# Attention tiles 5 to 8 of a forgetting-attention and mixture kernel: scores computed once with keys along the row, P transposed by DMA, the tail's products alternating between batches

## The chip, the cores and the metric

One core of a Trainium2 chip runs the whole kernel. The metric is the device time of one execution in microseconds (us). Three runs of the kernel before gave 1038.94, 1040.11 and 1040.14 us, median 1040.11. Engines: PE (matrix products, with PEld, its weight loads), DVE (VectorE), ACT (ScalarE), POOL (GpSimd) and SP (here mainly the queue that issues DMAs).

## The reference

Causal attention with a forget bias, then a mixture of eight experts whose routing weights are balanced in eight rounds, then a bilinear layer:

```python
B, H, S, D = 2, 8, 576, 64
scores = (q @ k.T) / sqrt(D)
cum = cumsum(maximum(s, 0))                       # along the sequence
scores = where(causal, -1e9, scores + minimum(-(cum_q - cum_k), 0))
attn = exp(scores - max(scores)); attn /= sum(attn) + 1e-9
x = (attn @ v) laid out as (1152 tokens, 512)
P = exp(x @ w_gate - max); 8 rounds of row and column normalising
x = sum over e of P[:, e] * (relu(x @ w1[e]) @ w2[e])        # 8 experts
out = ((x @ w_a) * (x @ w_b)) @ w_out
```

## The kernel before

The 1152 tokens are nine tiles of 128 rows. Tiles 0 to 3 are batch 0, tiles 4 to 7 batch 1 (576 = 4 x 128 + 64), and tile 8, the tail, holds the last 64 rows of both batches, batch 0 on partitions 0 to 63 and batch 1 on 64 to 127. The order of the tiles is 0, 4, 1, 2, 3, 5, 6, 7, 8. Nearly every factor is held as a sum of two f16 numbers (hi and lo), and a product is three f16 products: hi hi, hi lo, lo hi.

Tiles 0 and 4 take `first_tile` (f32 products of 64 rows, L1033, four heads in each half of the array's rows). The others take this path:

- `k_prep` and `q_prep` write split keys and queries, and DMA transposes on SP's queue (L792, L810, L816) turn them into `ka1`, `ka2`, `b3` and `b4`, with head dimension and bias terms on the partitions.
- `row_max` computes approximate scores with queries on the partitions and keys along the row: one product a head over all its keys (L838; in the tail L855 and L868), and a mask product on the diagonal block (L823). DVE takes the row maxima (L842, L859, L871).
- `shift` (L885 to L896) turns the maxima into two more rows of `b3`: three small DVE operations, a transpose on PE, two copies by ACT.
- `probs` computes the scores a second time, now with keys on the partitions, so that P comes out transposed: two products of 128 queries for each block of 128 keys and head (L932, L933), four blocks in one bank `st`. ACT takes exp (L942). In tiles 3 and 5 to 8 (`SEL`) POOL zeroes what lies above the diagonal (L946). The result is split into hi (L954, L953) and lo (L956, L957) in one of five `pt` buffers. `pv` multiplies by v: three products of 64 or 65 columns a block (L975 to L977), into `xp`. The last column of v is 1 and gives the row sum.
- `x_tile` divides by the sum, splits and transposes by DMA (L1098) into `xt`. `gate_item` computes the eight routing logits of a tile in 12 products (L1135 to L1137).

The tail runs `probs` for one batch after the other, its last keys as blocks of 64 rows.

Expert 0 (`e0_tile`: L1179 to L1181 and L1199 to L1201) runs between these pieces, tile by tile, whenever the attention's next piece isn't ready. After the last attention tile, `switch` gives the attention's memory to experts 1 to 7. The weights of expert 1, in two stage buffers by then, are squared and summed (L593) and split only after it, since their units lie in that memory.

The order on each engine is static. `Graph.schedule` plans it when the kernel is built: each operation has a cost, an engine or a choice of engines, its dependencies and a rank, and of those that can start soonest on an engine the lowest rank goes first. `GROUPS` holds an offset for the ranks of each group ("m5" is row_max of tile 5, "p5" its probs). An engine works through its list in order and waits where an operand isn't there yet. SP's queue is in order as well.

Of the kernel before, what the change touches and what calls it, by code (L numbers as in the profile page):

```python
# [252 lines left out]
def forgetting_attention_moe_bilinear_kernel(  # L253
# [50 lines left out]
    wgs = const.tile([128, 2, KD, E], F16, name="wgs")  # L304
# [110 lines left out]
    mx8 = ap.tile([128, H], F32, name="mx8")  # L415
    ush = ap.tile([128, H], F32, name="ush")
# [91 lines left out]
    def vone(b):  # L508
        g.add("POOL", 200, lambda: nc.gpsimd.memset(vs[b][:, :, :, 64:66], 1.0), w=[("vone", b)] + ([("v1r", j) for j in range(NBLK)] if b else []), rank=0.7)
# [60 lines left out]
    def w_prep(name, e, unit_ids, rank, fine=False, rel=0.0, zs=None, srank=None):  # L570
# [7 lines left out]
        for u in range(2):  # L578
            z = next_stage() if zs is None else zs[u]
            sts.append(z)  # L580
            sv = stage[z].rearrange("p (c f) -> p c f", c=4)
            src = src0[u].rearrange("(c p) f -> p c f", p=128)
            step = 4 // npc
            for c in range(0, 4, step):
                g.add("DMA" if fine else "SP", 650 * step, lambda qu=nc.sync, sv=sv, src=src, c=c, step=step: qu.dma_start(
                    out=sv[:, c:c + step], in_=src[:, c:c + step]),
                    w=[("st", z, cc) for cc in range(c, c + step)], rank=rank + u * 0.01, rel=rel)
# [43 lines left out]
    def v_prep(b, rank, rel=0.0):  # L631
# [8 lines left out]
        g.add("DVE", 60, lambda: nc.vector.memset(mxs, 0.0), w=[("vm", b)], rank=0)  # L640
        for j in range(NBLK):
            kr = 128 if j < NJ else vrem
            g.add("DMA", 1080 * kr / 128, lambda q, j=j, kr=kr: q.dma_start(
                out=sv[j][0:kr].rearrange("p (h d) -> p h d", h=H),
                in_=v[b, :, j * 128:j * 128 + kr, :].rearrange("h s d -> s h d")), w=svk[j], rank=rank, rel=rel)
            g.add("ACT", 800, lambda j=j, kr=kr: sumsq(mxs[0:kr, j:j + 1], sv[j][0:kr], junk[0:kr]), r=svk[j] + [("vm", b)], w=[("vmx", b, j)], rank=rank)
# [7 lines left out]
        for j in range(NBLK):  # L654
            kr = 128 if j < NJ else vrem
# [14 lines left out]
    def qk_load(name, t, b, rank, rel=0.0):  # L670
        src, dst, keys = rawof[name]
        for (tt, p0, rows, bb, s0) in segs:
            if tt == t and bb == b:
                g.add("DMA", 1080 * rows / 128, lambda qu, p0=p0, rows=rows, s0=s0: qu.dma_start(
# [3 lines left out]
    SK, SQ, IK, IQ, ESC, AL, IAL, CF, NAF, APL, TA, TB = range(12)  # L678
# [4 lines left out]
    def scales(b, rank):  # L683
# [38 lines left out]
        def consts2():  # L722
# [11 lines left out]
            nc.vector.scalar_tensor_tensor(out=col(APL), in0=col(NAF), scalar=2.0 ** 10, in1=col(APL), op0=ALU.mult, op1=ALU.add)  # L734
            r = slice(64 * b, 64 * b + 64)
            nc.vector.tensor_copy(cst[r, 2, 0:TB + 1], cst[r, b, 0:TB + 1])
# [244 lines left out]

    fsc = {}

    def first_load(t, rank):
        b = t // NJ
        for name in "kq":
            qk_load(name, t, b, rank)
        g.add("DMA", 1080, lambda q: q.dma_start(out=vf[:, :, 0:64], in_=v[b, :, 0:128, :].rearrange("h s d -> s h d")), w=["vf"], rank=rank + 0.02)
# [7 lines left out]
    def first_tile(t, rank):  # L996
# [3 lines left out]
        for gg in range(2):  # L1000
# [9 lines left out]
            g.add("PE", 1065, pre, r=["idb", "msk", "ones", ("bd", b, gg)], w=[("ss", y)], rank=rank, rows=0.2)  # L1010
        zt = []
        for src, keys, scale, pi in ((kraw[t], krk[t], 1.0, 2), (qraw[t], qrk[t], qk_scale, 3)):
# [8 lines left out]
            g.add("PE", 535, tr, r=keys + ["id32"], w=[("st", z)], rank=rank, rows=0.3)  # L1021
            g.add(("ACT", "DVE"), (600, 660), (lambda z=z, pi=pi, scale=scale: nc.scalar.activation(ptf[pi], st[z], AF.Copy, scale=scale),
                  lambda z=z, pi=pi, scale=scale: nc.vector.tensor_scalar(ptf[pi], st[z], scale, None, op0=ALU.mult)),
                  r=[("st", z)], w=[("pt", pi, 0), ("pt", pi, 1)], rank=rank)
        for gg in range(2):
            y, z = ys[gg], stc[0] % NST
            stc[0] += 1

            def mm(gg=gg, y=y):
                for w in range(4):  # L1030
                    r = slice(64 * gg, 64 * gg + 64)
                    c = slice(w * 128, w * 128 + 128)
                    nc.tensor.matmul(ss[y][:, w * 128:(w + 1) * 128], lhsT=ptf[3][r, c], rhs=ptf[2][r, c], start=False, stop=True, skip_group_check=True)  # L1033

            g.add("PE", 900, mm, r=[("pt", pi, x) for pi in (2, 3) for x in range(2)], w=[("ss", y)], rank=rank, rows=0.3)
# [12 lines left out]
            g.add("PE", 535, tr, r=[("p32", gg), "id32"], w=[("st", z)], rank=rank, rows=0.3)  # L1048
# [7 lines left out]
            g.add("PE", 860, pv, r=[("pt", gg, 0), ("pt", gg, 1), "vf", "vfone"], w=[("xp", gg)], rank=rank, rows=0.3)  # L1056
# [4 lines left out]
    def x_tile(t, rank):  # L1061
# [17 lines left out]
        if t in FIRST:  # L1079
# [7 lines left out]
            g.add("PE", 535, tr, r=["id32"], w=[("st", z)] + xbk, rank=rank, rows=0.3)  # L1087
# [16 lines left out]
    def gate_prep(rank):  # L1104
# [6 lines left out]
        g.add("ACT", 215, lambda: hi_of(wgs[:, 0].rearrange("p c e -> p (c e)"), wf, sx), r=["wgn", ("wgsx",)], w=["wgs"], rank=rank)  # L1111
        g.add("DVE", 160, lambda: lo_of(nc.vector, wgs[:, 1].rearrange("p c e -> p (c e)"), wf, sx, wgs[:, 0].rearrange("p c e -> p (c e)")),
# [15 lines left out]
    def gate_item(t):  # L1128
# [4 lines left out]
        def mm():  # L1133
            for c in range(KD):
                nc.tensor.matmul(p, lhsT=xt[:, 0, c, sl], rhs=wgs[:, 0, c], start=(c == 0), stop=False)  # L1135
                nc.tensor.matmul(p, lhsT=xt[:, 0, c, sl], rhs=wgs[:, 1, c], start=False, stop=False)
                nc.tensor.matmul(p, lhsT=xt[:, 1, c, sl], rhs=wgs[:, 0, c], start=False, stop=(c == KD - 1))  # L1137

        g.add("PE", 310, mm, r=[("xt", t), "wgs"], w=mbk(m), rank=frank())
        g.add("DVE", 195, lambda: nc.vector.tensor_scalar(logit[:, t], p, isx[:, t:t + 1], gi_[0], op0=ALU.mult, op1=ALU.mult),  # L1140
# [132 lines left out]
    for t in TORD[2:]:  # L1273
# [15 lines left out]
        g.at = f"m{t}"  # L1289
        mxk = row_max(t, zb, u0)  # L1290
        shift(t, zb, mxk, u0)
        g.at = f"p{t}"
        probs(t, zb, u0 + 2)
# [779 lines left out]
LAND = 1100.0  # L2073
SEL = (3, 5, 6, 7, 8)
GROUPS = {
# [54 lines left out]
```

## Time and profile before

| | |
|---|---|
| Median of three runs | 1040.11 us |
| The profiled execution's own time | 1039.97 us |
| Its span from first to last instruction | 1038.2 us |
| Busy: PE, DVE, ACT, POOL | 98%, 74%, 53%, 9% of the span |
| DMA | 114.29 MB, mean 110 GB/s |

PE's busy time is an upper figure: its products are pipelined, so each one's listed duration (about 0.2 us) overlaps the next one's. What a product costs PE when products follow each other is the distance between the starts. The span has three stretches: up to about 125 us loads, preparations and the first attention tiles; to about 224 us the rest of attention with expert 0 between; then experts 1 to 7 and the bilinear layer.

### The profile page before, as it was taken

What the parts mean: (1) busy time and instruction counts of PE and PEld (TensorE: products, weight loads), DVE (VectorE), ACT (ScalarE), POOL (GpSimd) and SP (SyncE); (2) the same over time, 40 slices, a digit from 0 to 9 for tenths busy, and PEclk for the clock granted to TensorE, in tenths of its full rate; (3) what the DMA queues carried; (4) which work ended last, traced back from release to release, by engine and by line L of the source; (5) the groups of instructions that cost most, each with busy time, mean ns of one, the idle gap of its engine ahead of it and who ended that gap; (6) DMA issues with size and microseconds to landing.
All of it is one profiled execution on the core that took longest, in us unless ns stands there. A gap on an engine that the chain in (4) does not pass through costs nothing.

```text
span 1038.2 us, 19277 instructions
## 1 busy us (share of the span) xinstructions
PE 1015.9 (98%) x7802; PEld 651.0 (63%) x7802; DVE 773.2 (74%) x1615; ACT 545.1 (53%) x1015; POOL 92.4 (9%) x152
## 2 busy tenths in 40 slices
PE   7798999999999999999999999999999999999998
PEld 4577777866546745754764674576477464455777
DVE  7798976369966898894889789389978796666402
ACT  5767757556235635653663773466355454545220
POOL 0356822000000000000000000000000000000000
PEclk9999999999999999999999999999999999999999
DMA  9986941022023235313334522332544542222202
GB/s 231 201 138 104 166 80 23 12 83 81 1 82 122 82 122 195 110 63 122 123 107 149 198 76 75 124 120 89 203 162 168 158 92 82 88 101 97 82 21 71
DMA packets 123370, 114.29 MB, mean 110 GB/s; under 512 B 84736, under 2 KB 99072, under 8 KB 118672
## 3 DMA queue, kind: packets, MB, share of 16 engines
q1 hardware_dynamic: 120144, 112.25, 37.6%
q10 hardware_dynamic: 3136, 0.81, 0.5%
q8 instruction: 61, 1.00, 0.4%
q14 instruction: 29, 0.24, 0.1%
HBM read 79.22 MB, written 21.23 MB: 97 GB/s over the span
## 4 chain that ended last, share of the span: by engine, by line
PE 91%; DMA 3%; DVE 3%; SPq 2%; issue 1%; ACT 0%; POOL 0%; DVEq 0%; ACTq 0%; POOLq 0%
PE yb L1201 10%; PE yb L1200 10%; PE yb L1199 10%; PE yb L1585 5%; PE yb L1587 5%; PE yb L1586 5%; PE mb L1585 3%; PE mb L1587 3%; PE mb L1586 3%; PE yb L1816 2%; PE yb L1817 2%; PE yb L1815 2%; PE mb L1156 2%; PE mb L1158 2%; PE mb L1157 2%; PE mb L1816 1%
## 5 line engine op out<-in xcount | busy, mean ns | idle before, releaser
L1199 PE MATMUL yb<-wun,ht 128*128 128x512 f16 x504 | 191.0, 379 | 0.0
L1200 PE MATMUL yb<-wun,ht 128*128 128x512 f16 x504 | 191.0, 379 | 0.0
L1201 PE MATMUL yb<-wun,ht 128*128 128x512 f16 x504 | 191.0, 379 | 0.0
L1201 PEld LDWEIGHTS <-ht 128*128 128x128 f16 x504 | 49.3, 98 | 59.5
L1200 PEld LDWEIGHTS <-ht 128*128 128x128 f16 x504 | 49.3, 98 | 58.4
L1199 PEld LDWEIGHTS <-ht 128*128 128x128 f16 x504 | 49.3, 98 | 58.4
L381 DVE SCALAR_TENSOR_TENSOR wun<-stage,sc,wun 128x1024 f16<-128x1024 f32 (+1 forms) x70 | 76.6, 1117 | 8.6 <-ACT wun L367 8.4
L1585 PE MATMUL yb<-sx,wun 128*128 128x288 f16 x288 | 82.4, 286 | 0.0
L1586 PE MATMUL yb<-sx,wun 128*128 128x288 f16 x288 | 82.4, 286 | 0.0
L1587 PE MATMUL yb<-sx,wun 128*128 128x288 f16 x288 | 82.4, 286 | 0.0
L1645 DVE SCALAR_TENSOR_TENSOR acc<-yb,pe,acc 128x512 f32<-128x512 f32 x63 | 47.3, 750 | 41.5 <-PE yb L1201 40.7
L1586 PEld LDWEIGHTS <-wun 128*128 128x128 f16 x672 | 65.8, 98 | 17.8 <-issue 0.3
L1585 PEld LDWEIGHTS <-wun 128*128 128x128 f16 x672 | 65.8, 98 | 17.6
L367 ACT ACTIVATE wun<-stage,sc 128x1024 f16<-128x1024 f32 (+1 forms) x64 | 63.1, 1021 | 25.2 <-PE yb L1201 21.1
L1587 PEld LDWEIGHTS <-wun 128*128 128x128 f16 x672 | 65.8, 98 | 16.6
L364 ACT ACTIVATE jk<-stage 128x1024 f16<-128x1024 f32 x52 | 54.8, 1054 | 32.8 <-DMA stage<-in_moe_w_dram 32.2
L367 ACT ACTIVATE wun<-h,sc 128x1024 f16<-128x1024 f32 x36 | 40.8, 1144 | 43.7 <-DVE h L1436 18.5
L1595 ACT ACTIVATE ht<-yb 128x288 f16<-128x288 f32 x96 | 39.1, 408 | 33.1 <-PE yb L1587 32.5
L1585 PE MATMUL mb<-xt,wun 128*128 128x288 f16 x192 | 54.9, 286 | 0.1
L1587 PE MATMUL mb<-xt,wun 128*128 128x288 f16 x192 | 54.9, 286 | 0.0
L1586 PE MATMUL mb<-xt,wun 128*128 128x288 f16 x192 | 54.9, 286 | 0.0
L1179 PE MATMUL mb<-xt,wun 128*128 128x128 f16 x288 | 52.3, 225 | 0.0
(486 smaller groups left out, 2692.4 us busy)
## 6 DMA issues: line engine op xcount, KB each, us to landing
stage<-in_moe_w_dram SPq DMA_DIRECT2D x26, 1024.0 KB, 5.2
md<-wun SPq DMA_DIRECT2D x18, 1024.0 KB, 4.3
wun<-md SPq DMA_DIRECT2D x12, 1024.0 KB, 4.9
stage<-in_moe_w_dram SPq DMA_DIRECT2D x24, 256.0 KB, 4.6
mr<-in_moe_w_a_dram SPq DMA_DIRECT2D x12, 512.0 KB, 6.3
mr<-in_moe_w_b_dram SPq DMA_DIRECT2D x12, 512.0 KB, 4.0
mr<-in_moe_w_out_dram SPq DMA_DIRECT2D x12, 512.0 KB, 4.8
stage<-md SPq DMA_DIRECT2D x5, 1024.0 KB, 4.8
```

Of the source, the lines that this page charges most:

```text
L364: nc.scalar.activation(out, src, AF.Square, accum_out=dst)
L367: nc.scalar.activation(hi, src, AF.Copy, scale=scale)
L381: eng.scalar_tensor_tensor(out=lo, in0=src, scalar=scale, in1=hi, op0=ALU.mult, op1=ALU.subtract)
L1179: nc.tensor.matmul(p, lhsT=wh, rhs=xh, start=(c == 0), stop=False)
L1199: nc.tensor.matmul(pp, lhsT=hh, rhs=wh, start=(f == 0), stop=False)
L1200: nc.tensor.matmul(pp, lhsT=hh, rhs=wl, start=False, stop=False)
L1201: nc.tensor.matmul(pp, lhsT=hl, rhs=wh, start=False, stop=(f == KF - 1))
L1585: nc.tensor.matmul(p, lhsT=wh, rhs=xh, start=first and ch == 0, stop=False, skip_group_check=True)
L1586: nc.tensor.matmul(p, lhsT=wh, rhs=xl, start=False, stop=False, skip_group_check=True)
L1587: nc.tensor.matmul(p, lhsT=wl, rhs=xh, start=False, stop=ch == 1, skip_group_check=True)
L1595: g.add("ACT", 52 + 120 + CN / 1.2, lambda: nc.scalar.activation(hh(), src(), AF.Relu), r=bk, w=k0, rank=-5)
L1645: g.add("DVE", 663, lambda t=t, z=z: nc.vector.scalar_tensor_tensor(out=acc[:, t], in0=yb[z], scalar=pe[:, t, e:e + 1], in1=acc[:, t], op0 ...
```

## The change

- Tiles 5 to 8 (`ROWP`) take a new `row_path` in place of `row_max`, `shift` and `probs`. The full scores (both products) are computed once, with keys along the row, and masked in PSUM. DVE takes the maximum and a bias from it, ACT takes exp a head at a time with that bias, and the result is split into hi and lo. Both halves of a group go through one DMA transpose on SP into a "room", a part of `raw` that held q or k. `pv` reads from there. Scores alternate over four banks (`ss`, `st`).
- In the tail, each piece has both batches' products next to each other, in the two halves of the array's columns. The last 64 keys get a group of their own for all heads. In `vs` they are placed on the partition half that a head's transposed P has, with zeros elsewhere: so their v comes in two DMAs a batch, after a zero fill.
- `first_tile` issues its 16 products as one piece that alternates between the two row halves, where it had two pieces of 8.
- `gate_item` takes 8 products for 12 (hi times both halves of the gate in one product of 16 columns); DVE adds the halves.
- Costs in the plan (loads 1080 to 1200, some of PE's) and all offsets in `GROUPS` are new. The rest of the kernel is as before.

```diff
+ROWP = (5, 6, 7, 8,)
 ...
+        if t in ROWP:
+            row_path(t, zb, u0)
+        else: (row_max, shift, probs as before)
 ...
+    def row_path(t, zb, rank):
+        kc = NJ * 128 if tail else 128 * (j + 1)
+        G = 512 // kc
+        rooms = [x for x in (0, 2, 3, 4, 5, 1) if x in (0, 2) or x == 1 and tail or 3 <= x <= t - 2]
+        lhs = ((b3[zb], ka2), (b4[z4], ka1))
+        def parts(pi, p3, flat, room, rk, m):
+            hi, lo, src = flat[:, 0:m], flat[:, m:2 * m], p32[p3][:, 0:m]
 ...
+            g.add("SP", 1600 * m / 512, lambda: nc.sync.dma_start_transpose(out=room[:, 0:2 * m]..., in_=flat[:, 0:2 * m]), ...)
 ...
+            def mm(h0_=h0_, sb=sb):
+                for w in range(G):
+                    if tail:
+                        for x, (q_, ka) in enumerate(lhs):
+                            for bb in range(B):
+                                nc.tensor.matmul(sb[half[bb]], lhsT=q_[:, h, half[bb]], rhs=ka[:, h, bb * NJ * 128:(bb + 1) * NJ * 128], ...)
+                        continue
+                    for x, (q_, ka) in enumerate(lhs):
+                        nc.tensor.matmul(ps, lhsT=q_[:, h], rhs=ka[:, h, b * NJ * 128:b * NJ * 128 + kc], ...)
+                    mask_s(ps[:, kc - 128:kc], 128, 128)
+            def top(hs=hs, sb=sb):
+                nc.vector.tensor_reduce(out=mxr[:, t, hs], in_=sb..., op=ALU.max)
+                if tail:
+                    nc.vector.tensor_tensor(out=mxr[:, t, hs], in0=mxr[:, t, hs], in1=mx8[:, hs], op=ALU.max)
+                nc.vector.tensor_scalar(nbi[:, t, hs], mxr[:, t, hs], cc(ci, NES), 14.0 * math.log(2.0), op0=ALU.mult, op1=ALU.add)
+            def ex(h0_=h0_, sb=sb, p3=p3):
+                for w in range(G):
+                    nc.scalar.activation(p32[p3][:, c], sb[:, c], AF.Exp, scale=cc(ci, ESC), bias=nbi[:, t, h0_ + w:h0_ + w + 1])
+                def pv(h=h, w=w, room=room):
+                    for i in range(NJ if tail else j + 1):
+                        for lo, vl in ((0, 0), (0, 1), (1, 0)):
+                            for bb in range(B) if tail else (b,):
+                                nc.tensor.matmul(o, lhsT=p, rhs=vs[bb][:, i, h, 66 * vl:66 * vl + 65 - vl], ...)
 ...
     # first_tile
+        def mm():
+            for w in range(4):
+                for gg in range(2):
+                    nc.tensor.matmul(ss[ys[gg]][:, w * 128:(w + 1) * 128], lhsT=ptf[3][r, c], rhs=ptf[2][r, c], ...)
 ...
     # gate_item
+                nc.tensor.matmul(mb[m][:, 0:2 * E], lhsT=xt[:, 0, c, sl], rhs=wgs[:, c].rearrange("p z e -> p (z e)"), ...)
+                nc.tensor.matmul(p, lhsT=xt[:, 1, c, sl], rhs=wgs[:, c, 0], ...)
 ...
     # v_prep
+        g.add("POOL", 500, lambda: nc.gpsimd.memset(sv[NJ], 0.0), ...)
+            for y in range(1 if j < NJ else 2):
+                rows = slice(0, 128) if j < NJ else slice(64 * y, 64 * y + 64)
+                hs = slice(0, H) if j < NJ else slice(y, H, 2)
```

## Rows read from the trace of the kernel before

**Rows 1.** The page's busy time of each engine, share and instructions.
```profile
PE 1015.9 (98%) x7802; PEld 651.0 (63%) x7802; DVE 773.2 (74%) x1615; ACT 545.1 (53%) x1015; POOL 92.4 (9%) x152
```

**Rows 2.** The page's chain of work that ended last, by engine.
```profile
PE 91%; DMA 3%; DVE 3%; SPq 2%; issue 1%; ACT 0%; POOL 0%; DVEq 0%; ACTq 0%; POOLq 0%
```

**Rows 3.** Stretches: length, busy us (instructions) by engine, clock, DMA share, GB/s.
```profile
60.00:112.00 52.00, 47.62 (x654) 36.97 (x654) 46.59 (x123) 38.46 (x69) 35.13 (x46) 1.00 0.73 116
...
112.00:200.00 88.00, 86.09 (x1478) 69.25 (x1475) 61.27 (x120) 55.98 (x96) 27.64 (x43) 1.00 0.39 72
125.00:200.00 75.00, 75.00 (x1267) 58.95 (x1266) 48.44 (x100) 46.27 (x80) 16.81 (x30) 1.00 0.28 51
```

**Rows 4.** PE in order of time, tile 7: start, duration, line, product.
```profile
148.65 0.38 PE L838 MATMUL ss<-ka,b 128*128 128x512 f16 x1
148.86 0.22 PE L823 MATMUL ss<-msk,idb 128*128 128x128 f16 x1
148.92 0.38 PE L838 MATMUL ss<-ka,b 128*128 128x512 f16 x1
...
157.38 0.22 PE L932 MATMUL st<-b,ka 128*128 128x128 f16 x1
...
158.21 0.22 PE L933 MATMUL st<-b,ka 128*128 128x128 f16 x1
```

**Rows 5.** PE in order of time, the tail's pieces and what follows each.
```profile
151.12 0.22 PE L855 MATMUL ss<-ka,b 128*64 128x64 f16 x2
...
151.75 0.23 PE L1179 MATMUL mb<-xt,wun 128*128 128x128 f16 x1
...
158.36 0.62 PE L868 MATMUL ss<-ka,b 128*64 128x512 f16 x4
158.92 0.23 PE L1179 MATMUL mb<-xt,wun 128*128 128x128 f16 x1
...
181.87 0.20 PE L932 MATMUL st<-b,ka 128*128 128x64 f16 x1
...
182.44 0.21 PE L975 MATMUL xp<-vs,pt 64*64 64x65 f16 x1
...
183.85 0.21 PE L975 MATMUL xp<-vs,pt 64*64 64x65 f16 x1
...
184.05 0.22 PE L975 MATMUL xp<-vs,pt 128*64 128x65 f16 x1
...
184.55 0.21 PE L975 MATMUL xp<-vs,pt 64*64 64x65 f16 x1
```

**Rows 6.** PE in order of time, the gate of tile 8 and what follows.
```profile
199.75 0.17 PE L1135 MATMUL mb<-wgs,xt 128*128 128x8 f16 x1
...
200.06 0.38 PE L1199 MATMUL mb<-wun,h 128*128 128x512 f16 x1
```

**Rows 7.** PE in order of time, eight products of a first tile.
```profile
43.04 2.07 PE L1033 MATMUL ss<-pt,pt 64*128 64x128 f32 x8
```

**Rows 8.** PE's waits for DMAs from 60 to 205 us: total, times, longest.
```profile
PE ss L838 <- DMA b<-qa: 0.3, 1, 0.3
...
PE mb L1135 <- DMA xt<-xhl: 0.2, 1, 0.2
```

**Rows 9.** Transposes of the keys: issue ns min/median/max on SP's queue, and issue to landing.
```profile
L792 SPq DMA_TRANSPOSE ka<-kn x18: 1232/1276/2606, 54.0 to 131.9; - x18
...
DMA to landing us min/median/max: 3.1/3.9/6.2
```

**Rows 10.** DVE from 112 to 205 us, a small operation: busy, mean ns, idle before.
```profile
L1071 DVE TENSOR_SCALAR rs<-xp 128x4 f32<-128x4 f32 x10 | 1.6, 160 | 5.9 <-PE xp L977 5.9
```

**Rows 11.** After the last attention tile: ACT, DVE and PE in order of time.
```profile
199.39 0.63 ACT L593 ACTIVATE wun<-stage 128x512 f16<-128x512 f32 x1 [2.72 <-DMA xt<-xhl]
...
211.50 3.39 DVE L381 SCALAR_TENSOR_TENSOR wun<-stage,sc,wun 128x512 f16<-128x512 f32 x5
...
224.65 0.34 PE L1156 MATMUL mb<-xt,wun 128*128 128x384 f16 x1
```

More of the change, by code (lines that the diff above doesn't have):

```diff
@@ L415, in forgetting_attention_moe_bilinear_kernel @@
     mx8 = ap.tile([128, H], F32, name="mx8")
+    nbi = ap.tile([128, NTL, H], F32, name="nbi")
     ush = ap.tile([128, H], F32, name="ush")
@@ L508, in vone, with f @@
     def vone(b):
-        g.add("POOL", 200, lambda: nc.gpsimd.memset(vs[b][:, :, :, 64:66], 1.0), w=[("vone", b)] + ([("v1r", j) for j in range(NBLK)] if b else []), rank=0.7)
+        def f():
+            nc.gpsimd.memset(vs[b][:, :, :, 64:66], 1.0)
+            for y in range(2):
+                nc.gpsimd.memset(vs[b][64 - 64 * y:128 - 64 * y, NJ, y::2, 64:66], 0.0)
+        g.add("POOL", 400, f, w=[("vone", b)] + ([("v1r", j) for j in range(NBLK)] if b else []), rank=0.7)
     vone(0)
@@ L640, in v_prep @@
         g.add("DVE", 60, lambda: nc.vector.memset(mxs, 0.0), w=[("vm", b)], rank=0)
+        g.add("POOL", 500, lambda: nc.gpsimd.memset(sv[NJ], 0.0), w=svk[NJ] + [svk[NJ][0] + ("b",)], rank=rank, rel=rel)
         for j in range(NBLK):
[L642 to L645, printed above, removed]
+            kr = 128
+            for y in range(1 if j < NJ else 2):
+                rows = slice(0, 128) if j < NJ else slice(64 * y, 64 * y + 64)
+                hs = slice(0, H) if j < NJ else slice(y, H, 2)
+                g.add("DMA", 1200 if j < NJ else 500, lambda q, j=j, rows=rows, hs=hs: q.dma_start(
+                    out=sv[j][rows].rearrange("p (h d) -> p h d", h=H)[:, hs],
+                    in_=v[b, hs, j * 128:j * 128 + rows.stop - rows.start, :].rearrange("h s d -> s h d")), w=svk[j] if y == 0 else [svk[j][0] + ("b",)], rank=rank, rel=rel)
+            if j == NJ:
+                svk[j] = [svk[j][0], svk[j][0] + ("b",)]
             g.add("ACT", 800, lambda j=j, kr=kr: sumsq(mxs[0:kr, j:j + 1], sv[j][0:kr], junk[0:kr]), r=svk[j] + [("vm", b)], w=[("vmx", b, j)], rank=rank)
@@ L673, in qk_load @@
             if tt == t and bb == b:
-                g.add("DMA", 1080 * rows / 128, lambda qu, p0=p0, rows=rows, s0=s0: qu.dma_start(
+                g.add("DMA", 1200 if rows == 128 else 900, lambda qu, p0=p0, rows=rows, s0=s0: qu.dma_start(
                     out=dst[t][p0:p0 + rows].rearrange("p (h d) -> p h d", h=H), in_=src[b, :, s0:s0 + rows, :].rearrange("h s d -> s h d")),
                     w=keys[t] if rows == 128 else [keys[t][b]], rank=rank, rel=rel)
-    SK, SQ, IK, IQ, ESC, AL, IAL, CF, NAF, APL, TA, TB = range(12)
+    SK, SQ, IK, IQ, ESC, AL, IAL, CF, NAF, APL, TA, TB, NES, LNC = range(14)
     def cc(ci, i, r=slice(0, 128)):
@@ L987, in first_load @@
             qk_load(name, t, b, rank)
-        g.add("DMA", 1080, lambda q: q.dma_start(out=vf[:, :, 0:64], in_=v[b, :, 0:128, :].rearrange("h s d -> s h d")), w=["vf"], rank=rank + 0.02)
+        g.add("DMA", 1200, lambda q: q.dma_start(out=vf[:, :, 0:64], in_=v[b, :, 0:128, :].rearrange("h s d -> s h d")), w=["vf"], rank=rank + 0.02)
     def first_scale(t, rank):
@@ L1008, in pre @@
                 nc.tensor.matmul(ss[y], lhsT=ones[0:H], rhs=bd[b][gg], start=False, stop=False, skip_group_check=True)
-            g.add("PE", 1065, pre, r=["idb", "msk", "ones", ("bd", b, gg)], w=[("ss", y)], rank=rank, rows=0.2)
+            g.add("PE", 1300, pre, r=["idb", "msk", "ones", ("bd", b, gg)], w=[("ss", y)], rank=rank, rows=0.2)
         zt = []
@@ L1024, in first_tile @@
                   r=[("st", z)], w=[("pt", pi, 0), ("pt", pi, 1)], rank=rank)
+        def mm():
+            for w in range(4):
+                for gg in range(2):
+                    r = slice(64 * gg, 64 * gg + 64)
+                    c = slice(w * 128, w * 128 + 128)
+                    nc.tensor.matmul(ss[ys[gg]][:, w * 128:(w + 1) * 128], lhsT=ptf[3][r, c], rhs=ptf[2][r, c], start=False, stop=True, skip_group_check=True)
+        g.add("PE", 1100, mm, r=[("pt", pi, x) for pi in (2, 3) for x in range(2)], w=[("ss", y) for y in ys], rank=rank, rows=0.2)
         for gg in range(2):
@@ L1027, in first_tile @@
             stc[0] += 1
[L1029 to L1035, printed above, removed]
             s3 = lambda y=y: ss[y].rearrange("p (h k) -> p h k", h=4)
@@ L1134, in mm, with ev @@
             for c in range(KD):
[L1135 to L1140, printed above, removed]
+                nc.tensor.matmul(mb[m][:, 0:2 * E], lhsT=xt[:, 0, c, sl], rhs=wgs[:, c].rearrange("p z e -> p (z e)"), start=(c == 0), stop=(c == KD - 1),
+                                 skip_group_check=True)
+                nc.tensor.matmul(p, lhsT=xt[:, 1, c, sl], rhs=wgs[:, c, 0], start=False, stop=(c == KD - 1), skip_group_check=True)
+        def ev():
+            q = mb[m][:, 0:2 * E].rearrange("p (z e) -> p e z", z=2)
+            nc.vector.tensor_reduce(out=logit[:, t], in_=q, axis=AX.X, op=ALU.add)
+            nc.vector.tensor_scalar(logit[:, t], logit[:, t], isx[:, t:t + 1], gi_[0], op0=ALU.mult, op1=ALU.mult)
+        g.add("PE", 210, mm, r=[("xt", t), "wgs"], w=mbk(m), rank=frank())
+        g.add("DVE", 320, ev,
               r=mbk(m) + ([("isx1", t)] if t in FIRST else [("isx", b) for b in tile_c(t)[1]]) + [("wgsx", "i")], w=[("logit", t)], rank=-5)
@@ L1288, in forgetting_attention_moe_bilinear_kernel @@
         zb = q_prep(t, u0 - 8)
[L1289 to L1293, printed above, removed]
+        if t in ROWP:
+            row_path(t, zb, u0)
+        else:
+            g.at = f"m{t}"
+            mxk = row_max(t, zb, u0)
+            shift(t, zb, mxk, u0)
+            g.at = f"p{t}"
+            probs(t, zb, u0 + 2)
         g.at = f"x{t}"
```

113 lines of the change are left out of this document (103 added, 10 removed), and 25 rows, old and new, of the table GROUPS.

## The prediction

> **What bounds the kernel now.** I read the page's busy times first, then the chain, then the stretches, and only then single products. PE is busy for 98% of the span [rows 1], and the chain that ended last is PE for 91% [rows 2]: the reader is to see that no single wait sets the end, PE's amount of work does. That is an average, so the stretch of the change is read by itself [rows 3]. From 125 to 200 us, where tiles 6, 7 and 8 and most of tile 5 run, PE is busy in all 75.00 us of 75, with DVE at 48.44 and ACT at 46.27. Before that, from 60 to 112 us, PE has 47.62 us of 52 and DVE 46.59: there DVE and loads also bind. So a product taken out behind 112 us is worth its whole time, as long as the other engines keep up in a shorter stretch. The listed duration of a product overlaps its neighbours'; the price is the distance between starts.
>
> **Tiles 5 to 7.** Removed are the transposed scores: 8 heads, two products, 2, 3 and 4 blocks, so 32 + 48 + 64 = 144 products of 128 columns. Sixteen of them start between 157.38 and 158.21 us, 15 distances, 0.055 us each [rows 4]: 144 x 0.055 = 7.9 us. Added is the second row product, 8 a tile. With 512 columns it takes 148.86 - 148.65 = 0.21 us (the mask behind it 0.06, there in both kernels) [rows 4]; for 384 and 256 columns I estimate in proportion 0.16 and 0.11. 8 x (0.21 + 0.16 + 0.11) = 3.8 us. The products with v stay, three a block. The four `shift` transposes of tiles 5 to 8 go, at the 0.06 us of a 128-column product 0.2 us. Net **-4.3 us**.
>
> **The tail.** Before [rows 5]: the last keys' 32 row products take 151.75 - 151.12 = 0.63 us. The 16 row products over 512 keys take 0.56 us in fours, so 2.2. Transposed scores take 182.44 - 181.87 = 0.57 us a group, ten groups: 5.7. Products with v take 184.55 - 183.85 = 0.70 us a batch and head, sixteen times: 11.2. In all 19.7 us. Here is the point of the alternation: a batch's fifteen products with v are 64 columns wide and follow each other in one half of the array, with a switch of shape between the three of the last keys (0.20 us) and the other twelve (0.50 us). The 32 row products, whose halves alternate, cost 0.63 / 32 = 0.020 us each, with the way in; the row products of 512 columns cost 0.14 each in a four, where 0.21 is the price alone.
>
> After: the last keys' scores are 48 products (two for one, and the mask): 48 x 0.020 = 0.95 us. Eight heads of four row products at 0.56: 4.5. Products with v, 24 a head in alternating halves: 24 x 0.020 = 0.47, eight times 3.8. The last keys' 48 products with v: 0.95. In all 10.2 us. Net **-9.5 us**. From below, if the products with v overlap no better than the twelve in one half, 0.50 / 12 = 0.042 each with the switch: 8 x 1.0 + 2.0 for 3.8 + 0.95, and the net is -4.2; on the other side, if they overlap as well as the 512-column ones, two thirds (0.14 of 0.21) of 0.020: 0.013 each, 1.6 us less, -11.1. I take the alternating row, since its shape is the same: 128 rows, 64 columns of the array, 64 moving.
>
> A rule speaks against it. Trainium skill, TensorEngine Tiling (Array Packing), Performance Considerations, Instruction Overhead: each product carries some 60 cycles, however few its columns, so that a dimension already small gives nothing. At 2.4 GHz that is an estimate of 25 ns, and the tail would give some 1.5 us less. The gate's 8-column products agree with it (0.026 us, the next part), the alternating row at 0.020 does not.
>
> **The gate.** Twelve products take 200.06 - 199.75 = 0.31 us, 0.026 each though they have 8 columns [rows 6]; eight take 0.21, also with 16 columns. Nine tiles: **-0.9 us**. DVE's added sum (an operation of 0.16 us [rows 10]) lies beside PE; only the routing at the end of expert 0 waits for the last.
>
> **The first tiles.** Eight f32 products of half the rows take 2.07 us [rows 7], four such pieces. Alternating row halves may overlap, which no row shows: from 0 to -4.1 us if both do fully; and if they don't overlap, the first half's maximum waits 2.07 us longer in each tile, +4.1 at worst. PE has idle time there, so even a full overlap is not wholly gained. I take **-1.0 us**. The new costs and offsets of the plan, the tail's v in two loads and its zero fill act ahead of 112 us as well. PE's unused time from 60 to 112 us is 4.4 us [rows 3]; a better order could at most take that, a worse one I bound by the same: -4.4 to +4.4, value 0, because nothing in the rows says which.
>
> **What the new path asks of the others.** Twenty-nine groups (4, 8, 8, 8 and 1) each make a transpose on SP's queue, where a key transpose holds the queue 1.28 us and lands after 3.1 to 6.2 us [rows 9]. From a group's scores to its product with v there are now a maximum, a bias, exp, hi, lo and that landing, so about 3 to 6 us more than before. Expert 0's products cover this, if the plan has placed enough of them ahead of the waiting `pv`, for PE's list is in order: behind a `pv` that waits, expert 0 waits too, and so do x, its transpose and the gate. On SP the transpose waits for `lo`, and behind it the preparations' transposes and expert 1's loads. How PE fared with such operands before: two waits, 0.5 us in all [rows 8], over 18 key transposes alone. For 29 that is 0.8 us; at the longest single wait each, 29 x 0.3 = 8.7 us.
> DVE gets a bias operation a group (28) and a maximum a group in the tail (8), 36 x 0.16 = 5.8 us [rows 10], and loses shift's. The stretch from 112 to 200 us shrinks by some 14.7 us, to 73, and DVE's 61.27 + 5.8 = 67 fill 91% of it. That is what DVE had from 60 to 112 us (46.59 of 52), where PE reached 92% [rows 3]: 8% of 73 is 6 us. Against this stands POOL, busy 27.64 of 88 and free of the diagonal's masking in these tiles, and able to take lo. I give back **+2.0 us**, nearer the low end, because in 125 to 200 us PE had no idle time at all with DVE at 65%.
>
> **What is late next.** Expert 1's weights are read only after the last attention transpose: ACT starts on them at 199.39, DVE's last split ends at 211.50 + 3.39 = 214.9, and their first product is at 224.65 [rows 11]. Those 9.8 us are slack. The first product moves forward by 14.7 us, so the last attention tile must land at least 4.9 us earlier than now. With 19.7 us of tail replaced by 10.2 it should.
>
> **Sum.** -4.3 - 9.5 - 0.9 - 1.0 + 2.0 = -13.7 us. The profiled execution took 1039.97 us, its span 1038.2 with 1.8 around it, and lies 0.14 below the median. 1039.97 - 13.7 = **1026.3 us**. Expert 1 onward has no change and PE stays its bound, so it only moves forward.
>
> **Rivals.**
> *The halves don't overlap in the products with v.* Each needs another weight load, while half of the 32 products in the row that overlaps share one constant weight, that of the mask. At the price of one half with the switch the tail gives 4.2 instead of 9.5: 1031.6 us. The skill's rule gives a milder form of it, some 1028. Against it: the row products over 512 keys overlap too.
> *DVE or the round trips become the bound.* Give-back 8.7 instead of 2.0: 1033 us. For it: DVE at 91%; tile 5 has only three rooms, one of them free only when the tail's keys are prepared. Against it: POOL's free time.
> *Slower: PE stops at `pv` in every group.* The plan counts a landing shorter than it is, `pv` stands too early in PE's list, and each of the 29 groups stops PE. From 15.7 / 29 = 0.54 us a group the gain is gone (15.7 being all gains); at 1.0 us a group, a quarter of the median landing, the time is 1039.97 - 15.7 + 29 = 1053 us. For it: 3.1 us is the shortest landing, and in tile 5's first part, from 112 to 125 us, the DMAs are full: (0.39 x 88 - 0.28 x 75) / 13 = 1.0 [rows 3]. Against it: the plan was able to hold waits for transposes at 0.5 us before [rows 8].
> *The front gains as well:* full overlap in the first tiles and a better order, -7 more: 1019 us.
>
> **How the numbers follow.** Forecast 0.56 (its own range 1022 to 1030), halves without overlap 0.12, DVE or round trips 0.15, slower 0.11, front 0.06. Of the third, 0.03 may end within 0.2% of before, which is about 2 us and what a measurement can tell here; of the slower case 0.01. So faster 0.86, same 0.04, slower 0.10. The range is 1018 to 1036: it takes in the front, the missing overlap and a give-back of 8.7 with a worse front, and leaves out the slower case and the edges, some 0.17.
>
> **What would show it.** Right: the first product of expert 1 some 13 to 15 us ahead of 224.65; products with v of the tail at about 0.5 us for 24; no wait of PE for a room above a microsecond in total per tile. Wrong: PE idle before the new `pv` with a DMA into `raw` as the releaser; DVE above 90% from 112 us on with PE idle beside it; 24 tail products taking 0.75 us or more; expert 1's split ending later than PE's last product of expert 0.

## The result, and the profile after

| | before | after |
|---|---|---|
| median (range), four runs each | 1039.53 us (1038.92 to 1040.14) | 1026.51 us (1024.9 to 1026.69) |
| profiled execution, span | 1039.97, 1038.2 | 1024.9, 1023.0 |
| first product of expert 1 starts | 224.65 | 208.78 |
| PE busy, idle until then | 206.43, 18.22 | 189.49, 19.29 |
| ACT starts the sums of expert 1's weights | 199.39 | 194.64 |

The ratio is 0.9871, with a 95% interval of 0.9854 to 0.9888: 13.0 us less by medians, 15.1 by the profiled executions (that of after is the shortest of its four). The forecast was 1026.3, in 1018 to 1036. The gain lies ahead of expert 1: its first product starts 224.65 - 208.78 = 15.87 us earlier, and what follows takes 814.22 us, 0.67 more than before.

The page of the kernel after: busy times, the clock in 40 slices, and the chain that ended last, by engine.

```profile
PE 999.6 (98%) x7514; PEld 631.2 (62%) x7514; DVE 771.1 (75%) x1652; ACT 549.3 (54%) x1020; POOL 78.5 (8%) x130
...
PEclk9989999999999999999999999999999999999999
...
PE 88%; DVE 3%; DMA 2%; issue 1%; POOL 1%; ACT 1%; POOLq 0%; ACTq 0%; SPq 0%; DVEq 0%
```

PE has 288 products fewer and 16.3 us less busy time than in [rows 1]; the shares hardly move. So the stretches must be read, in the columns of [rows 3]; the first ends where expert 1's first product starts.

```profile
0.00:208.78 208.78, 189.49 (x2347) 137.38 (x2348) 161.73 (x436) 149.90 (x288) 64.48 (x99) 0.98 0.83 153
...
60.00:112.00 52.00, 48.91 (x632) 36.48 (x632) 43.79 (x121) 38.80 (x69) 24.33 (x37) 0.96 0.68 118
112.00:208.78 96.78, 95.87 (x1463) 69.59 (x1461) 68.12 (x163) 67.99 (x121) 22.17 (x25) 1.00 0.78 129
...
112.00:185.00 73.00, 72.35 (x1150) 52.57 (x1147) 57.71 (x136) 54.51 (x90) 22.17 (x25) 1.00 1.01 166
```

From 112 us on PE is idle for 0.91 us of 96.78, where before it was idle for 1.91 of 88 [rows 3]: the new path cost PE no idle time there. DVE fills 57.71 / 73 = 79% of its part, not 91%. The DMA share is new: it is the mean busy share of the core's sixteen DMA engines, so at 1.01 they are listed as busy all the time, where before it was 0.39. PE hardly had to wait for it, as the rows below show; nor is 1.01 a ceiling, since a run below shows 1.45.

PE in order of time, after: a head of the tail's products with v, then the last keys', each with the product behind it.

```profile
171.79 0.57 PE L1105 MATMUL xp<-vs,raw 128*64 128x65 f16 x24
172.30 0.23 PE L1334 MATMUL mb<-xt,wun 128*128 128x128 f16 x1
...
187.71 0.95 PE L1125 MATMUL xp<-vs,raw 128*64 128x65 f16 x48
188.60 0.23 PE L1334 MATMUL mb<-xt,wun 128*128 128x128 f16 x1
```

24 products take 0.51 us and 48 take 0.89, where 0.47 and 0.95 stood in the sum. The transposes into the rooms and the products that read them, after: instructions with duration in ns (min/median/max), first and last start; then what these waited for, and the time from issue to landing.

```profile
L1035 SPq DMA_TRANSPOSE raw<-pt x29: 1215/1274/2239, 125.8 to 182.1; - x29
...
DMA to landing us min/median/max: 2.8/3.3/5.3
```

```profile
L1105 PE MATMUL xp<-vs,raw x408: 190/194/218, 129.2 to 186.1; 128*128 128x65 f16 x72, 128*64 128x65 f16 x32, 128*64 128x64 f16 x32
...
  DMA raw<-pt: 0.2, 1
```

A room's transpose lands like a key's [rows 9], and PE waited for one once, 0.2 us. The plan placed the products late enough.

The end of the attention after, on ACT, DVE and PE, against [rows 11].

```profile
194.64 0.63 ACT L599 ACTIVATE wun<-stage 128x512 f16<-128x512 f32 x1 [2.56 <-DMA xt<-xhl]
...
204.56 5.39 DVE L381 SCALAR_TENSOR_TENSOR wun<-stage,sc,wun 128x512 f16<-128x512 f32 x8
...
208.14 0.81 PE L1795 MATMUL yb<-xt 128*128 128x512 f16 x3
208.78 0.33 PE L1311 MATMUL mb<-xt,wun 128*128 128x384 f16 x1
```

The slack is used up: DVE's splits end at 204.56 + 5.39 = 209.95, behind the first product that uses the first of them (before, 9.8 us ahead of it). So one of the prediction's signs of being wrong is there, a last split that ends later than PE's last product of expert 0 (which starts at 207.92); but PE has no gap ahead of 208.78, and this cost it nothing. The last attention tile came 199.39 - 194.64 = 4.75 us earlier, and 4.9 had been the need.

### The profile page after: what moved, and what is told of

Same layout as the page of the kernel before. It is cut to its first block, busy times and chain, and to the rows that moved or that the text cites. A ratio compares the mean times of both kernels' runs of the same rounds, so it can differ in the third digit from the quotient of the medians.

```text
span 1023.0 us, 18802 instructions
## 1 busy us (share of the span) xinstructions
PE 999.6 (98%) x7514; PEld 631.2 (62%) x7514; DVE 771.1 (75%) x1652; ACT 549.3 (54%) x1020; POOL 78.5 (8%) x130
## 4 chain that ended last, share of the span: by engine, by line
PE 88%; DVE 3%; DMA 2%; issue 1%; POOL 1%; ACT 1%; POOLq 0%; ACTq 0%; SPq 0%; DVEq 0%
PE yb L1355 11%; PE yb L1354 11%; PE yb L1356 11%; PE yb L1743 5%; PE yb L1745 5%; PE yb L1744 5%; PE mb L1743 3%; PE mb L1745 3%; PE mb L1744 3%; PE yb L1973 2%; PE yb L1975 2%; PE yb L1974 2%; PE mb L1311 2%; PE mb L1313 2%; PE mb L1312 2%; PE mb L1975 2%
## 5 line engine op out<-in xcount | busy, mean ns | idle before, releaser
L367 ACT ACTIVATE wun<-h,sc 128x1024 f16<-128x1024 f32 x36 | 40.8, 1145 | 43.4 <-DVE h L1594 18.5
L1753 ACT ACTIVATE ht<-yb 128x288 f16<-128x288 f32 x96 | 39.0, 408 | 32.8 <-PE yb L1745 32.3
```

The costliest lines, as they stand in the source:

```text
L367: nc.scalar.activation(hi, src, AF.Copy, scale=scale)
```

## The experiments

My theory: PE lost 14 to 17 us of products, the round trips are covered, and nothing else is left to spare. Rivals: the first tiles or the tail's alternation are not what pays; PE was about to stop at the rooms; the new order alone makes the gain. In each, "first product" is the start of expert 1's first product; before it is 224.65, after 208.78.

**First tiles: the row halves one after the other.**

```diff
-            for w in range(4):
-                for gg in range(2):
+            for gg in range(2):
+                for w in range(4):
```

> The changed kernel with the 16 products of a first tile in the same piece, but one row half after the other instead of alternating. Theory (PE's work counts, also in the front): the alternating piece took 2.08 us for 16, so each piece goes back to about 4.1 us, twice; part of it falls into time in which PE waits anyway: 1 to 4 us more than the changed kernel's 1026.5, so 1027.5 to 1030.5. Rival (loads and DVE set the front, PE has time to spare there): within 0.5 us of 1026.5.

Measured: 1026.85 us (1024.09 to 1027.07), ratio 0.9871 [0.9855, 0.9888]. PE in order of time, sixteen alternating products of after and what follows; the same sixteen here, one half after the other; then the stretch to the first product here.

```profile
42.86 2.08 PE L1180 MATMUL ss<-pt,pt 64*128 64x128 f32 x16
44.88 0.29 PE L1334 MATMUL mb<-xt,wun 128*128 128x128 f16 x1
```

```profile
42.69 3.09 PE L1180 MATMUL ss<-pt,pt 64*128 64x128 f32 x16
45.71 0.29 PE L1334 MATMUL mb<-xt,wun 128*128 128x128 f16 x1
```

```profile
0.00:209.42 209.42, 192.47 (x2348) 140.79 (x2349) 162.50 (x436) 149.56 (x288) 64.43 (x99) 0.98 0.83 152
```

Sixteen alternating products take 2.08 us, what eight of one half took [rows 7]: the overlap is complete. One half after the other takes 3.09 (the other first tile's piece as well), not the 4.1 that I had expected: in one piece the halves overlap in part in this order too. So per tile the change took 2 x 2.07 - 2.08 = 2.1 us of products from PE, half of it by alternating and half by making one piece of two. Undone, PE is busy 3.0 us more up to the first product, 2.0 of them in these two pieces, and idle 2.3 us less, and the time stays. The rival was right: there PE has time to give, and the alternation earns nothing. What one piece in place of two earns, no run shows.

**The tail's products with v, batch after batch.**

```diff
-                            for bb in range(B) if tail else (b,):
+                    for bb in range(B) if tail else (b,):   # outermost; pv_tail likewise
```

> The changed kernel, but the tail's products with v run batch after batch instead of alternating (same pieces, same order of pieces). Theory (the halves overlap, and PE's work counts one for one): 24 products go from 0.51 us to 24 x 0.031 + 0.13 = 0.88 us, eight times, and the last keys' 48 from 0.88 to 1.6: 3.7 us more, 1030.2 us. Rival (attention waits for round trips or DVE, PE has slack): within 1 us of 1026.5. Second rival (the rule of a fixed cost per product, 25 ns, with or without alternation): no change of the pieces' length at all.

Measured: 1028.43 us (1027.03 to 1029.13), 0.9891 [0.9876, 0.9906]. PE in order of time: one head, and the last keys.

```profile
171.37 0.85 PE L1105 MATMUL xp<-vs,raw 128*64 128x65 f16 x24
172.16 0.23 PE L1334 MATMUL mb<-xt,wun 128*128 128x128 f16 x1
...
189.32 1.61 PE L1125 MATMUL xp<-vs,raw 128*64 128x65 f16 x48
190.86 0.23 PE L1334 MATMUL mb<-xt,wun 128*128 128x128 f16 x1
```

24 in one half after the other take 0.79 us, 0.033 each, against 0.021 alternating: 8 x 0.28 and 1.54 - 0.89 for the last keys make 2.9 us, where 3.7 had been expected. The medians show 1.9: the runs of the two kernels don't overlap, the 95% intervals still do. The alternation is worth somewhat less than the rest of what the edit does to the products with v: before, one batch's fifteen took 0.70 [rows 5], 1.40 for a head, where 24 in one half take 0.79. With a head's share of the last keys (1.54 / 8 = 0.19) that is a fall of 0.42 from treating these apart, and with it from having no switch of shape in each head; the alternation adds 0.28 + 0.65 / 8 = 0.36. That the switch is what the 0.42 is made of shows in the starts before: within a shape they are mostly 0.03 us apart, at each switch 0.12 or 0.13, from these two products to the next ones in [rows 5].

```profile
183.72 0.19 PE L977 MATMUL xp<-vs,pt 128*64 128x65 f16 x1
...
183.93 0.19 PE L977 MATMUL xp<-vs,pt 64*64 64x65 f16 x1
```

Two switches a batch and head, some 0.09 us each above an ordinary distance, are 0.37 of the 0.42; this is an estimate, since no run undoes the switch alone.

The Trainium skill, TensorEngine Tiling (Array Packing), Performance Considerations, Instruction Overhead, would have some 25 ns for each product in either order (an estimate from its 60 cycles at 2.4 GHz); the trace shows less alternating and more in one half, and the row decides.

**Each room's transpose twice.**

```diff
-            g.add("SP", ..., lambda: nc.sync.dma_start_transpose(...)
+            g.add("SP", ..., lambda: [nc.sync.dma_start_transpose(...) for _ in range(2)]
```

> The changed kernel with each of the 29 transposes into a room issued twice, one behind the other. Theory (round trips are covered by expert 0's products; PE waited 0.2 us for rooms): landings come 1.3 to 4 us later, cover mostly holds: 1026.5 to 1030. Rival (the DMAs are the next bound: their share was 1.0 from 112 to 185 us): 29 x 1.3 us more of the queue, 1040 to 1065 us.

Measured: 1109.07 us (1106.77 to 1109.83), 1.0665 [1.0648, 1.0682]: far outside both. PE's waits from 110 to 290 us (total, times, longest), and SP's for its own landings.

```profile
PE xp L1105 <- DMA raw<-pt: 43.4, 18, 9.9
PE ss L1070 <- ACT p L1091: 11.7, 2, 7.1
```

```profile
SPq L1035 <- DMA raw<-pt: 54.4, 29, 3.6
```

The second write into a room carries a wait for the semaphore of the first one's landing, so this doubled the round trip and blocked the queue for 54.4 us, instead of loading the queue a little. It doesn't tell my two theories apart as meant; it does show the slower rival's mechanism at work: once the rooms come late, PE stops at `pv` behind them.

**Tile 7's eight transposes also to memory that nobody reads.**

```diff
+            to = [room] + ([cps[cpc[0] % 3]] if t in SPARE else [])   # SPARE = (7,)
-  lambda: nc.sync.dma_start_transpose(out=room...)
+  lambda: [nc.sync.dma_start_transpose(out=x...) for x in to]
```

> The changed kernel with each of tile 7's eight transposes issued a second time, into memory that nothing reads (old key buffers), so that no copy waits for another's landing as in the run with each room written twice. Theory now (the attention's end has only about 1.5 us to spare before the first product of expert 1, and SP's queue is what paces the attention behind 125 us): 8 x 1.4 us = 11 us more of the queue, less what the queue has in gaps, 1032 to 1038 us, PE idle in front of the tail's products with v or of expert 1. Rival (as predicted: round trips are covered and some 5 us are to spare): 1026 to 1029 us.

Measured: 1035.81 us (1032.4 to 1039.22, ten runs), 0.9969 [0.9955, 0.9983], as the theory had it. Stretches, PE's waits from 112 to 216 us, and who waited for the transposes (here, then after).

```profile
150.00:175.00 25.00, 20.59 (x283) 12.64 (x281) 16.91 (x41) 13.56 (x21) 3.48 (x3) 0.93 1.04 175
175.00:185.00 10.00, 7.32 (x157) 5.63 (x156) 6.67 (x16) 5.48 (x10) 0.00 (x0) 1.00 1.45 174
```

```profile
PE ss L1073 <- ACT p L1094: 3.2, 1, 3.2
PE xp L1108 <- DMA raw<-pt: 2.9, 2, 2.7
```

```profile
  ACT pt L1031: 11.6, 8
```

```profile
  ACT pt L1030: 0.8, 2
```

Eight transposes more, for whose result nobody waits, cost 9.3 us, 1.2 each, about the 1.27 us that each holds SP's queue. They keep the copy of P (`pt`) longer, so that ACT waits 11.6 us in place of 0.8 before it can write the next one; PE idles 7.1 of the 35 us, the attention ends at 202.22, 7.6 later, and so does the first product (216.39). There is no slack in the row path: eight transposes more on SP's queue, and it is slower than PE's work beside it. Whether the queue, the transfers themselves (the DMA share rises from 1.16 to 1.45 in 175 to 185 us) or the number of `pt` buffers binds isn't told apart.

**Parts of the path, and the old order.** One line each: `ROWP` lists the tiles that take the row path, and the last kernel has the `GROUPS` of before. The plan is made anew for each set.

```diff
-ROWP = (5, 6, 7, 8,)
+ROWP = (5, 6, 7)      # then (8,), then ()
```

> The changed kernel with only tiles 5 to 7 on the row path, the tail on the old one (its last keys' v lie where the new path wants them, so the tail's output is off; the work is the old one's). Theory (the tail gives 9.5 of the 14.7 us): 1036 us, 1034 to 1040. Rival (the gain is the row path's scores of tiles 5 to 7 or the front): 1030 us or less.

> The changed kernel with only the tail on the row path, tiles 5 to 7 on the old one. Theory (tiles 5 to 7 give 4.3 us of products): 1031 us, up to 6 more by the offsets: 1030 to 1037. Rival (the twenty transposes of tiles 5 to 7 take from the other engines what they give PE): 1027 us or less.

> The changed kernel with no tile on the row path (the tail's output is off, since its last keys' v lie where the new path wants them; the work is the old one's), but with the new offsets, first tiles, gate and loads. Theory (the gain is the row path's products; the offsets alone give nothing): 1026.5 + 13.8 = 1040 us, up to 6 more because the offsets were made for another set of pieces. Rival (the new order of the front carries the gain): 1032 us or less.

```diff
-    "m5": (71060.0, 0.0), "m6": (-15160.0, 1000.0), ...
+    "m5": (11460.0, 400.0), "m6": (570.0, 1000000.0), ...   # all of GROUPS from before
```

> The changed kernel planned with the offsets of the kernel before; everything else of the change stays. Theory (the gain is products taken from PE; the new offsets serve to keep other engines in time): between 1026 and 1034 us. Rival (the gain comes from the new order): 1037 us or more.

| kernel | median (range) | ratio | first product |
|---|---|---|---|
| tiles 5 to 7 alone, new offsets | 1040.78 (1039.51 to 1041.5) | 1.0009 [1.0, 1.0019] | 225.27 |
| tail alone, new offsets | 1050.79 (1050.4 to 1051.68) | 1.0107 [1.0092, 1.0122] | 234.40 |
| neither, new offsets | 1056.24 (1055.47 to 1058.4) | 1.0162 [1.0144, 1.0179] | 240.22 |
| both, old offsets | 1045.0 (1042.51 to 1048.37) | 1.006 [1.0038, 1.0081] | 225.99 |

The stretch to the first product in each, in the same order.

```profile
0.00:225.27 225.27, 199.95 (x2480) 148.58 (x2480) 165.58 (x432) 151.70 (x294) 65.11 (x102) 1.00 0.73 140
```

```profile
0.00:234.40 234.40, 198.35 (x2474) 146.37 (x2474) 169.84 (x435) 147.45 (x283) 69.06 (x116) 0.96 0.64 125
```

```profile
0.00:240.22 240.22, 207.97 (x2602) 158.22 (x2603) 169.88 (x429) 149.00 (x287) 65.93 (x110) 0.96 0.55 112
```

```profile
0.00:225.99 225.99, 196.07 (x2347) 141.63 (x2348) 167.52 (x429) 142.68 (x275) 86.00 (x119) 0.95 0.77 141
```

The reader is to compare stretch and PE's busy time. With the tail undone PE is busy for 199.95 - 189.49 = 10.5 us more, near the 9.5 forecast for it (the clock is 1.00 in one and 0.98 in the other), but the time rises by 14.3: idle time goes from 19.3 to 25.3. With the tail alone, neither, or the old offsets, idle time is 36.1, 32.3 and 29.9 us, and the granted clock falls to 0.95 or 0.96, so part of the busy time there is slower products. All four expectations were missed: 1034 to 1040 for tiles 5 to 7 alone (by 0.8), 1030 to 1037 for the tail alone, 1040 to 1046 for neither and 1026 to 1034 for the old offsets, since I took the offsets for neutral. The new order is no gain by itself (1056 us without the path), and the path without it loses (1045). What the row path is worth with an order made for a part of it, no run shows; so the gain can't be shared out between tiles and tail.

**Fillers against the clock's fall.** The granted clock of after fell for some microseconds, which I had not foreseen. Stretches of after, the clock as third column from the end.

```profile
54.00:56.00 2.00, 1.04 (x9) 1.02 (x9) 2.00 (x5) 2.00 (x5) 0.00 (x0) 1.00 1.12 215
...
58.00:60.00 2.00, 1.69 (x17) 1.31 (x17) 1.93 (x6) 2.00 (x5) 1.19 (x3) 0.50 0.72 149
60.00:62.00 2.00, 1.78 (x10) 1.37 (x10) 1.96 (x5) 1.28 (x4) 1.92 (x3) 0.50 1.59 142
62.00:64.00 2.00, 2.00 (x8) 0.87 (x7) 2.00 (x4) 1.15 (x3) 1.74 (x3) 0.50 1.00 220
```

From 57.7 to 64.5 us it is 0.50, 1.2 of 2.4 GHz, after a stretch in which PE was busy for about half and waited for DVE. Before, the clock row of 60 to 112 us says 1.00 [rows 3], but that is one execution: of the twenty of the kernel before that ran beside the runs with spare transposes and old offsets, five have a mean clock of 1.000 and the others 0.996 to 0.999. So a fall somewhere is not new with the change. Four kernels put products that nobody reads into the gaps.

```diff
+            for _ in range(WARM.get(i, 0)):
+                nc.tensor.matmul(xp[1][:, 456:512], lhsT=idb, rhs=msk[0][:, 0:56], ...)   # 56 columns
+WARM = {188: 6, 194: 6, 237: 40, 261: 20}   # before that: 104, by the plan's gaps, all before 38 us
...
+                nc.tensor.matmul(ss[1], lhsT=idb, rhs=msk[0]..., ...)                      # 512 columns
+WARM = {190: 2, 196: 3, 237: 5, 261: 3}     # last: also 97: 2, 100: 1, 143: 1, 214: 1, 182: 3
```

> The changed kernel with small products (128 rows, 56 columns, into a corner of a PSUM bank that nothing reads) put into PE's list wherever the plan has a gap before 75 us; about 200 of them, the order of all else unchanged. Theory (the granted clock of 0.5 from about 57 to 64.5 us, after a stretch in which PE was little busy, costs 3 to 4 us of the changed kernel's gain): clock 1.00 in that stretch, 1022 to 1025 us. Rival (the front is bound by loads and DVE, the clock there costs nothing): within 1 us of 1026.5, or slower by what the products delay.

> The changed kernel with 72 small products that nothing reads, put right ahead of the four pieces before which PE sat idle between 50 and 58.5 us (6, 6, 40 and 20 of them); the earlier filling put its products where the plan had gaps, and PE stayed as idle as before from 52 to 56 us. Theory (idle PE there lets the clock fall to 0.5 from about 57 to 64.5 us): the clock stays at 1.00 and the time falls by 2 to 4 us, 1022.5 to 1024.5 us. Rival (DVE, busy 4.9 of 5 us there, and loads set the front): 1026 to 1028 us with the clock at 1.00.

> The changed kernel with 13 products of 128 rows and 512 columns that nothing reads (into a score bank that is free by then), ahead of four pieces between 51 and 58.5 us (2, 3, 5 and 3). The small fillers of the run before left the clock at 0.5 from 55 to 65 us although PE was listed busy throughout, so they didn't test it. Theory (the clock's fall costs part of the gain): clock at 1.00 or a shorter fall, 1023 to 1025.5 us. Rival (DVE is busy nearly without a gap from 40 to 68 us and sets the pace there): 1026 to 1028.5 us even where the clock stays up.

> Leaves nothing out of the result; adds nine more 512-column products, whose results nobody reads, at the places between 31 and 38.5 us where PE waits, beside the thirteen of the wide fill. Theory: products at 39 to 48 us cost 0.107 us a distance in both earlier kernels because PE had been idle for much of 22 to 39 us; with the fillers they cost near 0.055 there, the front ends 1 to 3 us earlier and the median is 1021.5 to 1023.5 us. Rival: DVE (8.4 of 9 us busy from 39 to 48 us) and the loads set the front, PE's price there costs nothing: 1023.5 to 1026.5 us, as with the wide fill alone (1024.45).

Measured: by the plan's gaps 1027.68 us (1026.26 to 1028.23), 0.9883 [0.9869, 0.9898]; 72 small ones where PE really waits 1027.56 (1025.28 to 1028.49), 0.9886 [0.9865, 0.9907]; thirteen wide ones 1024.45 (1022.91 to 1026.43), 0.9859 [0.984, 0.9878]; with nine more ahead of them 1028.13 (1024.97 to 1029.22), 0.9893 [0.9874, 0.9912]. Stretches of the kernel with 72 small ones, and of the one with thirteen wide ones.

```profile
55.00:60.00 5.00, 5.00 (x53) 4.91 (x51) 2.39 (x9) 4.41 (x9) 2.01 (x3) 0.50 0.86 170
60.00:65.00 5.00, 5.00 (x52) 4.41 (x52) 4.64 (x11) 2.65 (x7) 4.41 (x5) 0.50 0.83 160
```

```profile
56.00:58.00 2.00, 2.00 (x17) 1.62 (x17) 1.86 (x8) 1.97 (x4) 1.86 (x3) 1.00 1.21 116
58.00:60.00 2.00, 1.93 (x23) 1.37 (x22) 1.93 (x6) 2.00 (x4) 0.67 (x1) 1.00 0.62 122
...
0.00:206.90 206.90, 187.81 (x2361) 135.43 (x2361) 161.77 (x436) 149.51 (x288) 64.61 (x99) 1.00 0.83 155
```

The small fillers miss their aim in the profiled executions: those by the plan's gaps all ran before 38 us, and with the 72 PE is listed as busy throughout and the clock is 0.50 all the same. With the wide ones the clock stays at 1.00, the first product comes 1.88 us earlier, and the median is the lowest of all and within that theory's range; but its runs overlap those of after. The kernel with nine more fillers missed both its theory and its rival. Its profiled clock is 1.00 too, but in its three other executions the mean is 0.995 to 0.998, so it is no counterexample. Over the four kernels, the seven executions with a mean clock of 1.000 took 1022.91 to 1027.95 us (median 1024.97), the nine with less 1026.26 to 1029.22 (1027.8). The executions of after, at 0.994 to 0.997, took no longer than 1026.69, so the fillers seem to cost something themselves. That the clock's fall costs some 2 us is therefore likely and not shown. The last kernel tells something else.

Stretch 39 to 48 us of after, and of the kernel with nine more fillers.

```profile
39.00:48.00 9.00, 9.00 (x76) 7.95 (x75) 8.42 (x36) 8.57 (x20) 4.60 (x10) 1.00 0.98 193
```

```profile
39.00:48.00 9.00, 5.39 (x78) 4.65 (x75) 8.20 (x35) 8.39 (x21) 4.40 (x9) 1.00 0.95 193
```

Nearly the same products (78 and 76) cost 5.39 us in place of 9.00, and the 3.6 us turned into idle time: DVE, at 8.2 to 8.4 of 9 us in both, sets the front. That fits the alternation in the first tiles, which earned nothing either.

Why the price halves, the clock column doesn't say: it reads 1.00 in both. But the trace holds no record of the clock ahead of 47.44 us in after (52.89 before, 37.91 with nine more fillers), and a stretch without a record prints as 1.00. At the first record the distance of starts falls; after, two neighbours ahead of it and two behind:

```profile
42.30 0.31 PE L1335 MATMUL mb<-xt,wun 128*128 128x128 f16 x1
42.41 0.31 PE L1336 MATMUL mb<-xt,wun 128*128 128x128 f16 x1
...
48.09 0.22 PE L1335 MATMUL mb<-xt,wun 128*128 128x128 f16 x1
48.15 0.22 PE L1336 MATMUL mb<-xt,wun 128*128 128x128 f16 x1
```

So by the distances PE ran at the lower clock there, before as well as after.

## Why the prediction was right

- **PE bounds from 112 us on.** Right: 95.87 of 96.78 us busy.
- **Tiles 5 to 7, tail and gate, -14.7 together.** Right in kind, a little small. Counted from each start to the next, up to the first product of expert 1, the products of attention and gate outside the first tiles cost PE 66.05 us before and 50.99 after: -15.1. In that, 24 products of after ran in the slow stretch from 57.7 us and took 2.91 us; at the full clock it would be some -16.5 (an estimate, with half of the 2.91). The tail's new pieces sum to 8 x 0.56 + 0.88 + 8 x 0.51 + 0.89 = 10.3 us; 10.2 was forecast. Alternating halves cost 0.019 to 0.021 us a product, so the rival without overlap and the milder rule both fall: batch after batch still gives 1028.4, since the 0.042 that I had put on a product in one half had the switch in it, and 0.032 to 0.033 is right.
- **First tiles, -1.0.** Wrong in its reason. The overlap is full, and the pieces went from 8.0 to 4.0 us by their starts; but PE's idle time ahead of 112 us rose by 2.1 us, and the alternation's half of the saving is worth nothing within what the runs can tell.
- **Give-back, +2.0.** Mis-sized. In PE's idle time behind 112 us it is 0.91 - 1.91 = -1.0, where I had given back 2.0. I added 5.8 us for DVE to its old time of the stretch; in fact DVE has 57.71 us in 112 to 185, where 61.27 stood for 112 to 200. The removed operations of `shift` had no price in my sum, and the plan moved work among stretches. The bias itself (28 of 0.216 us, 6.0) was about as forecast.
- **DVE or round trips as the bound.** Not so here: 0.2 us of waiting for rooms. But it is near: eight spare transposes bring 9.3 us. The price that I had put on a round trip had no ground: the two waits of [rows 8] were for transposes of queries and of x, and I divided them by the 18 of the keys.
- **Slower, PE stops at `pv`.** It didn't. That late rooms stop PE there is shown by the doubled transposes (43.4 us); that the order alone can bring it about is not. With the old offsets the same instructions are slower than before by 0.4 to 0.8%, but PE waited for rooms for 0.9 us in all at L1105. Of the 5.4 us between the spans of that kernel and of before, 1.3 lie ahead of the first product of expert 1 and 4.1 behind it (817.61 us against 813.55); what makes the latter I did not follow up.
- **What is late next.** Right: 4.9 us of advance needed, 4.75 had, and the splits now end 1.2 us behind the first product's start, without a gap in PE's work.
- **Not foreseen:** the clock's fall at 57.7 us, and that PE ran at the lower clock up to 47 us; the 2.07 us of [rows 7] is a price at that clock (the same sixteen alternating products take 1.16 us with the wide fillers, where the clock had risen just before).

In sum, up to the first product of expert 1: -15.1 for attention and gate, -4.0 for the first tiles' pieces, +2.1 for products that the change doesn't touch (they cost more where the clock is low), +1.1 of idle time, -15.9 in all; and +0.7 behind it. The forecast had -14.7, -1.0 and +2.0, -13.7 in all. The mechanism, PE's products behind 112 us taken out one for one, holds. That 1026.3 lies 0.2 from the median is luck: the first tiles' pieces gave 3 us more than their term and the give-back was 3 us too dear, against this stand 2.1 and 0.7 us and the front's idle time without a term, and the four runs of after are 1.8 us apart.

## What to carry to other kernels

Price the products that you take out by the distance of their starts, and look first at switches of shape: by the rows, treating the odd block apart gave somewhat more here than alternating the halves. The row path paid only with an order made for it: replan with the whole set of changes, and don't judge one part under another's order. Where another engine sets a stretch, quicker or fuller products in it show as idle time and not as a gain.

## What the runs showed of the hardware

- Two halves of the rows with f32 operands overlap fully when they alternate: sixteen products in 2.08 us, eight in one half in 2.07 [rows 7], sixteen one half after the other in 3.09, all at the lower clock.
- Products of 128 rows and 64 columns of the array, 64 or 65 columns moving, cost 0.019 to 0.021 us each with the two halves alternating, and 0.032 to 0.033 with one half after the other.
- A switch of shape between such products, 128 rows to 64 or back, shows as 0.12 or 0.13 us from start to start, where 0.03 is usual.
- With the 72 small fillers, from 55 to 65 us, PE is listed as busy for 10 of 10 us and the granted clock was 0.50: the listed busy time doesn't tell the clock.
- From 39 to 47 us of after, 128-column products start 0.107 us apart, twice the 0.055 of elsewhere. The clock's row reads 1.00 there, but the trace's first record of the clock is at 47.44 us, where the distance falls. With fillers ahead, the first record is at 37.91 us, and they are 0.055 apart at 38.5. So ahead of the first record the distance of starts tells the clock, and the row doesn't.
